# Decode attention over two caches: VectorE's work on the large cache as a hardware loop, each round's values loaded behind its own keys, strips summed in the loop

## The chip, the cores and the metric

The kernel runs on one core of a Trainium2 chip. The metric is the device time of one execution in microseconds (us). Between chips the kernel before moved from 1348.2 to 1349.3 us, so every experiment was timed beside runs of the kernel before on the same chip. All runs quoted are "fast", none of them over 1.5% above the fastest of its kernel.

Ratios are the mean time of one kernel's fast runs over that of the kernel before in the same rounds, so they are not quite the ratio of the medians that are quoted.

## The reference

Two independent attention blocks for a single query token, results concatenated. Block A ("the large cache") has 32 heads with 32 768 keys each; block B ("the small cache") has 32 query heads on 8 cache heads and looks at the last 4096 keys only.

```python
q = (x @ wq) per head                    # x: 1 x 512
scores = einsum("bhqd,bhkd->bhqk", q, k) * 128 ** -0.5
p = softmax(scores)
o = einsum("bhqk,bhkd->bhqd", p, v)
out = o.reshape(1, 1, 4096) @ wo         # A: 32 heads x 32768 keys; B: last 4096 keys, 8 cache heads
```

Every cache byte is used once: 2 x 268 MB for A, 2 x 8 MB for B, and four weight matrices of 4 MB, together 570 MB.

## The kernel before

In this kernel PE does the matrix products (19316 in the profiled run, its weight loads counted apart), VectorE and ScalarE the work on vectors (1664 and 169 instructions), GpSimd only some setting up (14), SyncE issues all loads but the two of x (1 KB each), and PSUM is the memory in which PE's results are placed.

The large cache is worked off in 32 rounds (16 pairs of heads, two halves of the keys each). One round needs two 4 MB loads of keys and two of values. There are two key buffers and two value buffers (slots), and all these loads are issued in order by SyncE. A round does this: PE transposes the keys in batches of eight 128x128 blocks, VectorE copies each batch out of PSUM, PE forms the scores; at the end of the round VectorE finds the maximum (a chain of about a dozen small operations), ScalarE takes the exponential, PE transposes the probabilities, ScalarE copies them, PE multiplies by the values, and VectorE adds the result to the running output, which lies in four strips of 32 partitions that have to be summed in the end.

In the kernel before this is software-pipelined: the value products of round i-1 run inside round i, so values are loaded one round behind their keys. PE's program is a hardware loop; VectorE's is straight code. The output weights are loaded last.

```python
WO_CUTS = {"A": (0, 16, 28, 32), "B": (0, 32)}        # pieces in which output weights are loaded
...
for i, (name, g, r) in enumerate(rounds):             # 32 rounds of the large cache
    self.loop = i if i >= 1 else None                 # a loop on PE only
    prev = [rounds[i - 1] + (u,) for u in range(2)]   # (i = 0: the small cache's two)
    for u in range(2):
        self.load_kv("k", name, g, r, u)              # keys of this round
        self.load_kv("v", *prev[u])                   # values of the round before
        hooks = {1: lambda: self.emit_PT(0)} if u == 0 else {}
        self.emit_unit(name, g, r, u, hooks)          # transposes, copies, scores
        self.emit_PV(*prev[u], pt=...)                # value products of the round before
    self.emit_round_end(name, g, r)                   # maximum, exponential
...
for u in range(2):
    self.load_kv("v", name, g, r, u)                  # values of the last round
for n in ("B", "A"):
    for part in range(len(self.WO_CUTS[n]) - 1):
        self.load_wo(n, part)
```

Of the kernel before, what the change touches and what calls it, by code (L numbers as in the profile page):

```python
# [9 lines left out]
DH = 128  # L10
# [26 lines left out]
class Op:  # L37
# [4 lines left out]



    __slots__ = ("eng", "fn", "deps", "take", "give", "loop", "signal", "count")

    def __init__(self, eng, fn, deps, take, give, loop):
        self.eng = eng
        self.fn = fn
        self.deps = [d for d in deps if d is not None]  # L50
        self.take = take
        self.give = give
        self.loop = loop
        self.signal = False
        self.count = None


class _Kernel:

    def __init__(self, nc, a, b, out):  # L60
# [30 lines left out]
        self.loop = None  # L91
# [3 lines left out]
    def op(self, eng, fn, *deps, take=(), give=None):  # L95
        o = Op(eng, fn, deps, list(take), give, self.loop if eng == "pe" else None)
        self.prog[eng].append(o)
        return o

    def build(self):  # L100
        nc = self.nc
        with nc.Block() as block:
            self.alloc()
            self.plan()
            for e in self.engines:
                for o in self.prog[e]:
                    for d in o.deps:
                        if isinstance(d, Op):
                            assert d.give is None
                            d.signal = True  # L110
            its = {}
            for o in self.prog["pe"]:
                if o.loop is not None:
                    assert not o.deps
                    its.setdefault(o.loop, []).append(o)
            for same in zip(*its.values(), strict=True):
                s = any(o.signal for o in same)
                for o in same:
                    o.signal = s
            for e in self.engines:  # L120
                n = 0
                for o in self.prog[e]:
                    if o.signal:
                        n += 1
                    o.count = n
            first = min(its) if its else None

            def emit_one(e, o, seen):
                need = {}
                for d in o.deps:  # L130
                    sem, val = (self.esem[d.eng], d.count) if isinstance(d, Op) else d
                    key = sem.name
                    if val > seen.get(key, 0) and val > need.get(key, (None, 0))[1]:
                        need[key] = (sem, val)
                for key, (sem, val) in need.items():
                    e.wait_ge(sem, val)
                    seen[key] = val
                for sem, n in o.take:
                    e.sem_inc(sem, -n)._wait_ge(sem, n)  # L139
                inst = o.fn(e)  # L140
                if o.give is not None:
                    inst.then_inc(o.give, 1)
                elif o.signal:
                    inst.then_inc(self.esem[o.eng], 1)

            def emit(eng_name):
                def body(e):
                    seen = {}
                    ops = self.prog[eng_name]
                    k = 0  # L150
                    while k < len(ops):
                        if ops[k].loop is None:
                            emit_one(e, ops[k], seen)
                            k += 1
                            continue
                        with e.Fori(0, len(its)):
                            for o in its[first]:
                                emit_one(e, o, seen)
                        k += sum(len(v) for v in its.values())
                return body  # L160

            block.gpsimd(emit("pool"))
            block.vector(emit("dve"))
            block.scalar(emit("act"))
            block.sync(emit("sp"))
            block.tensor(emit("pe"))

    def alloc(self):
# [6 lines left out]
        self.ptsb = [sb(f"ptsb{i}", [128, 512], BF16) for i in range(2)]  # L175
# [8 lines left out]
        for name, d in self.X.items():  # L184
# [3 lines left out]
                oc=sb(f"oc_{name}", [128, d["NG"], DH + 1], F32),  # L188
# [17 lines left out]
        self.qw = sb("qw", [128, 2, 64], BF16)  # L206
        ps = nc.alloc_psum_tensor
# [3 lines left out]
        self.ACC = [ps(f"psACC{i}", [128, 512], F32) for i in range(2)]  # L211
        s = nc.alloc_semaphore
        self.esem = {e: s(f"sem_{e}") for e in self.engines}
# [5 lines left out]
        self.t_copy = s("t_copy")  # L219
        self.t_exp = s("t_exp")  # L220
        self.t_q = s("t_q")
        self.t_pt = s("t_pt")
        self.t_acc = [s(f"t_acc{i}") for i in range(2)]
# [6 lines left out]
    def load_kv(self, which, name, g, r, u):  # L230
        d = self.X[name]
        slot = u if name == "A" else g
        buf, sem, free = ((self.kbuf, self.ksem, self.kfree) if which == "k" else (self.vbuf, self.vsem, self.vfree))
        h0 = g * d["kvg"] + u * d["kvu"]
        base = d["key0"] + d["blk"] * r
        src = d[which][0, h0:h0 + d["kvu"], base:base + d["blk"], :]
        src = src.rearrange("s (p j) d -> p s (j d)", p=128)
        dst = buf[slot][:, :].rearrange("p (s x) -> p s x", s=d["kvu"])
        self.load(dst, src, sem[slot], free[slot])

    def load_wq(self, name):
        slot = {"B": 0, "A": 1}[name]
        self.load(self.vbuf[slot][:, :], self.X[name]["wq"].rearrange("(p t) c -> p (t c)", t=4), self.vsem[slot],
                  self.vfree[slot])

    WO_CUTS = {"A": (0, 16, 28, 32), "B": (0, 32)}
    WO_SLOT = {"B": 0, "A": 1}

    def load_wo(self, name, part):
# [4 lines left out]
                  self.kfree[slot])  # L254
# [3 lines left out]
    def plan(self):  # L258
        self.kfree, self.vfree = [None, None], [None, None]
        self.nbatch = 0  # L260
        self.pending = []
        self.alphas = []
        self.fresh = True
# [8 lines left out]
        self.emit_unit("B", 0, 0, 0, {})  # L272
        self.emit_round_end("B", 0, 0)
        self.emit_unit("B", 1, 0, 0, {1: lambda: self.emit_PT(1)})
        self.emit_round_end("B", 1, 0)
        self.emit_qproj("A")
        self.emit_qcopy(0)

        rounds = [("A", i // a["R"], i % a["R"]) for i in range(self.NIT)]
        for i, (name, g, r) in enumerate(rounds):  # L280
            self.loop = i if i >= 1 else None
            if i == 0:
                prev = [("B", 0, 0, 0), ("B", 1, 0, 0)]
            else:
                prev = [rounds[i - 1] + (u,) for u in range(2)]
            for u in range(2):
                self.load_kv("k", name, g, r, u)
                self.load_kv("v", *prev[u])
                hooks = {1: lambda: self.emit_PT(0)} if u == 0 else {}
                self.emit_unit(name, g, r, u, hooks)  # L290
                self.emit_PV(*prev[u], pt=1 if i == 0 and u == 0 else 0)
            self.emit_round_end(name, g, r)
            if i + 1 < self.NIT:
                self.emit_qcopy(i + 1)
        self.loop = None
        name, g, r = rounds[-1]
        for u in range(2):
            self.load_kv("v", name, g, r, u)
# [3 lines left out]
        self.emit_PT(0)  # L302
        for n in ("B", "A"):
            self.emit_gather(n, 0, self.X[n]["NG"] - (n == "A"))
        self.emit_spread("B")
        for u in range(2):
            self.emit_PV(name, g, r, u, pt=0, final=True)
        self.emit_gather("A", a["NG"] - 1, a["NG"])
# [6 lines left out]
    def constants(self):  # L315
# [10 lines left out]
        for n in ("B", "A"):  # L326
            pool(lambda g, n=n: g.memset(c[n]["hsel"][:, :], 0.0))
            self.k_pool = pool(lambda g, n=n: g.memset(c[n]["b"][:, :], 0.0))
        dve = lambda fn, *deps, **k: self.op("dve", fn, *deps, **k)
        for i in range(2):  # L330
            dve(lambda v, i=i: v.memset(self.ACC[i][:, :], 0.0), give=self.t_acc[i])
# [18 lines left out]
    def emit_qproj(self, name):  # L350
        t = self.c[name]
        slot = {"B": 0, "A": 1}[name]
        ps, wq = self.ACC[slot], self.vbuf[slot]
# [8 lines left out]
        o = self.op("pe", mm, (self.xsem[name], 16), take=[(self.vsem[slot], 16), (self.t_acc[slot], 1)])  # L362
        self.vfree[slot] = o
        if name == "B":
            self.qready = self.op("dve", lambda v: v.tensor_copy(
                self.qz[:, 32:].rearrange("p (k w) -> p k w", w=32)[:, 0:8, 0:4],
                ps[:, 0:NQH].rearrange("p (k a) -> p k a", a=4)), o, self.k_pool)
        else:
            self.qready = self.op("dve", lambda v: v.tensor_copy(self.qa[:, :], ps[:, 0:NQH]), o)
        self.op("dve", lambda v: v.memset(self.m4[0:1, 0:1], 0.0), give=self.t_acc[slot])  # L370

    def emit_qcopy(self, i):
        g = i // self.X["A"]["R"]
# [230 lines left out]
```

## Time and profile before

Median 1348.19 us (1347.91 to 1348.41, three runs).

The kernel reads at 428 to 435 GB/s from the third slice to the 38th. At 432 GB/s, 570.4 MB take 1,320 us of the span of 1347.5 us.

The stage table of the end (columns: stretch, its length, busy us and instructions of PE, PE's weight loads, VectorE, ScalarE, GpSimd, then granted PE clock, DMA share, GB/s):

```profile
...
50.00:65.00 15.00, 7.35 (x166) 6.71 (x167) 5.46 (x19) 1.17 (x4) 0.00 (x0) 0.64 1.00 417
...
1295.00:1306.00 11.00, 8.41 (x238) 6.52 (x235) 9.47 (x24) 0.00 (x0) 0.00 (x0) 1.00 0.34 122
...
1333.00:1338.00 5.00, 5.00 (x22) 1.90 (x21) 0.00 (x0) 0.00 (x0) 0.00 (x0) 0.89 0.30 124
...
```

There is a hole (a stretch in which the mean DMA rate falls) between 1295 and 1306 us: 122 instead of 432 GB/s, which is 7.9 us of DMA time. It is there because SyncE's queue stands still at the last value load, whose buffer comes free only when the value product that starts at 1301.02 us is done, at 1303.0; the output weights, issued at 1303.39, stand behind it:

```profile
...
1301.02 1.96 PE L499 MATMUL psACC<-vbuf,ptsb 128*2 128x128 bf16 x128
...
1303.39 0.43 SPq L228 DMA_DIRECT2D kbuf<-in_B_wo_dram  x1
...
```

The timeline of one round (start, duration, engine, line, operation, tiles, count, and in brackets the idle time before it and what ended it):

```profile
...
623.34 3.57 PE L401 MATMUL psT<-ident,kbuf 128*128 128x128 bf16 x32 [7.37 <-PEq L139]
...
662.21 1.01 PE L401 MATMUL psT<-ident,kbuf 128*128 128x128 bf16 x8 [5.86 <-PEq L139]
```

The first transposes of two successive rounds' second halves are 38.87 us apart, which is four loads of 4.19 MB at 432 GB/s. Before each, PE stood idle (7.37 and 5.86 us; the sequencer, PEq, waited at the semaphore of the keys): the round waits for keys, and the kernel is bound by DMA. The end of the timeline:

```profile
...
1328.36 0.09 PEld L569 LDWEIGHTS psS<-kbuf,oz_B 128*1 128x1 bf16 x2 [2.73 <-DMA kbuf<-in_B_wo_dram]
...
1338.09 7.07 PE L569 MATMUL psPT<-kbuf,oz_A 128*1 128x512 bf16 x32
...
1345.20 0.68 DVE L573 CAST out_sb<-psPT 1x512 bf16<-1x512 f32 x1 [6.23 <-PE psPT L569]
```

The output projection of B starts when its 4 MB of weights have landed (1328.36), and that of A ends at 1345.2.

### The profile page before, as it was taken

The page shows a single profiled execution, that of the slowest core. Times are in us where ns is not written, and L with a number is a line of the kernel's source. Part 1 is how long each engine was busy: PE and PEld are TensorE (multiplying, and loading weights), DVE is VectorE, ACT ScalarE, POOL GpSimd, SP SyncE. Part 2 cuts the span into 40 slices and gives each one's busy share as a digit, 9 for nine tenths or more (in the row PEclk, how much of TensorE's full clock was granted, in tenths as well). Part 3 has the DMA queues.
Part 4 walks back from the last instruction along what each step waited for, and adds up shares of the span by engine and source line. Part 5 has one row for each costly group of instructions (what it writes and reads, how often), then busy time and mean ns, then how long its engine had stood idle before and what let it go on. Part 6 is the DMA issues. An engine that isn't in the chain of part 4 may idle for free. (4 is left out here: it accounts for less than half of the span.)

```text
span 1347.5 us, 42022 instructions
## 1 busy us (share of the span) xinstructions
PE 929.0 (69%) x19316; PEld 770.9 (57%) x19316; DVE 803.5 (60%) x1664; ACT 57.6 (4%) x169; POOL 2.0 (0%) x14
## 2 busy tenths in 40 slices
PE   3677766676577667667766775776677667667776
PEld 3556655565456556555655655565565556556553
DVE  3665755676565567556655765665675566557650
ACT  0000000000000000000000000000000000000000
POOL 0000000000000000000000000000000000000000
PEclk9888978888887888788878888877887888788778
DMA  9999999999999999999999999999999999999985
GB/s 400 422 429 428 431 433 429 433 432 432 429 433 432 433 430 430 434 432 430 432 432 431 431 433 432 431 430 433 432 433 428 434 432 430 430 435 431 431 337 254
DMA packets 21730, 570.81 MB, mean 424 GB/s; under 512 B 2498, under 2 KB 2500, under 8 KB 2628
## 3 DMA queue, kind: packets, MB, share of 16 engines
q1 hardware_dynamic: 21412, 570.44, 98.6%
q8 instruction: 15, 0.25, 0.1%
q14 instruction: 15, 0.12, 0.0%
q10 hardware_dynamic: 288, 0.00, 0.0%
HBM read 570.43 MB, written 0.00 MB: 423 GB/s over the span
## 5 line engine op out<-in xcount | busy, mean ns | idle before, releaser
L407 DVE COPY kt<-psT 128x1024 bf16<-128x1024 bf16 x1056 | 668.1, 685 | 385.6 <-PE psT L401 384.2
L401 PE MATMUL psT<-ident,kbuf 128*128 128x128 bf16 x8448 | 630.9, 245 | 370.3 <-PEq L139 366.0
L401 PEld LDWEIGHTS psT<-ident,kbuf 128*128 128x128 bf16 x8448 | 589.2, 112 | 469.3 <-issue 468.1
L431 PE MATMUL psS<-kt,qw 128*32 128x512 bf16 x2048 | 165.3, 401 | 0.0
L499 PE MATMUL psACC<-vbuf,ptsb 128*2 128x128 bf16 (+1 forms) x8256 | 132.1, 222 | 17.5 <-issue 14.9
L499 PEld LDWEIGHTS psACC<-vbuf,ptsb 128*2 128x2 bf16 (+1 forms) x8256 | 122.3, 85 | 35.6 <-issue 20.4
L466 ACT ACTIVATE psb<-psS,nb_A 128x512 bf16<-128x512 f32 x32 | 22.0, 688 | 971.6 <-DVE nb_A L464 971.6
L528 DVE SCALAR_TENSOR_TENSOR oc_A<-psACC,hot_A,oc_A 128x128 f32<-128x128 f32 x48 | 16.9, 351 | 62.9 <-PE psACC L499 62.9
L431 PEld LDWEIGHTS psS<-kt,qw 128*32 128x32 bf16 x2048 | 33.0, 96 | 25.4 <-issue 4.3
L482 ACT ACTIVATE ptsb<-psPT 128x512 bf16<-128x512 bf16 x34 | 20.3, 597 | 225.6 <-PE psPT L479 225.6
L451 DVE TENSOR_REDUCE tr_in<-psS 128x1 f32<-128x512 f32 x34 | 23.5, 691 | 4.5 <-PE psS L431 2.1
L453 DVE COPY m<-tr_a 1x16 f32<-1x16 f32 (+1 forms) x136 | 22.3, 164 | 2.6
L460 DVE COPY b_A<-mr_A 1x16 f32<-1x16 f32 x128 | 21.1, 165 | 2.4
L525 DVE TENSOR_SCALAR oc_A<-psACC,hot_A 128x128 f32<-128x128 f32 x16 | 5.6, 351 | 23.7 <-PE psACC L499 23.7
L479 PE MATMUL psPT<-ident,psb 128*128 128x128 bf16 x136 | 13.6, 224 | 4.3 <-PEq L139 4.3
L358 PE MATMUL psACC<-x_B,vbuf 128*128 128x1 bf16 x128 | 3.5, 165 | 13.6 <-PEq L139 13.6
L479 PEld LDWEIGHTS psPT<-ident,psb 128*128 128x128 bf16 x136 | 9.3, 100 | 4.7 <-issue 4.7
L569 PE MATMUL psS<-kbuf,oz_B 128*1 128x512 bf16 x32 | 9.9, 485 | 2.6 <-DMA kbuf<-in_B_wo_dram 2.6
L358 PEld LDWEIGHTS psACC<-x_B,vbuf 128*128 128x128 bf16 x128 | 3.5, 104 | 13.6 <-issue 13.6
L469 ACT ACTIVATE alpha_A<-cm_A,nb_A 128x1 f32<-128x1 f32 x32 | 9.0, 283 | 0.0
L569 PEld LDWEIGHTS psS<-kbuf,oz_B 128*1 128x1 bf16 x32 | 3.2, 102 | 8.9 <-issue 4.1
L573 DVE CAST out_sb<-psS 1x512 bf16<-1x512 f32 x1 | 0.7, 679 | 12.3 <-PE psS L569 12.3
(69 smaller groups left out, 104.6 us busy)
## 6 DMA issues: line engine op xcount, KB each, us to landing
kbuf<-in_A_k_cache_dram SPq DMA_DIRECT2D x64, 4096.0 KB, 27.9
vbuf<-in_A_v_cache_dram SPq DMA_DIRECT2D x64, 4096.0 KB, 35.3
kbuf<-in_B_k_cache_dram SPq DMA_DIRECT2D x2, 4096.0 KB, 27.7
vbuf<-in_B_v_cache_dram SPq DMA_DIRECT2D x2, 4096.0 KB, 25.5
vbuf<-in_B_wq_dram SPq DMA_DIRECT2D x1, 4096.0 KB, 12.5
vbuf<-in_A_wq_dram SPq DMA_DIRECT2D x1, 4096.0 KB, 41.7
kbuf<-in_B_wo_dram SPq DMA_DIRECT2D x1, 4096.0 KB, 24.9
kbuf<-in_A_wo_dram SPq DMA_DIRECT2D x1, 2048.0 KB, 29.3
```

The lines of the kernel that those rows point to most:

```text
L401: inst = e.transpose(T[:, 128 * k:128 * k + 128], src[:, DH * tile:DH * tile + DH], self.ident[:, :])
L407: self.op("dve", lambda v: v.tensor_copy(KT[:, :], T[:, :]), o, give=self.t_copy)
L431: inst = e.matmul(self.S[32 * c:32 * c + 32, :], lhsT=win, rhs=self.kt[(bb + c // 2) % NKT][:, 512 * (c % 2):512 * (c % 2) + 512], start=f ...
L451: o = dve(lambda v: v.reduce_max(tr["in"][:, 0:1], self.S[:, :], axis=AXX), sdone, self.k_pool)
L453: cps = [dve(lambda v, c=c: v.tensor_copy(m4[0:1, W * c:W * c + W], tr["a"][32 * c:32 * c + 1, 0:W]), o) for c in range(STRIPS)]
L460: x = dve(lambda v, c=c: v.tensor_copy(t["b"][32 * c:32 * c + 1, 0:W].rearrange("p (k h) -> p k h", k=KC), t["mr"][0:1, k, :].unsqueeze(1) ...
L466: self.op("act", lambda s: s.activation(out=self.psb[:, :], in_=self.S[:, :], func=ACTF.Exp, bias=t["nb"][:, k:k + 1], scale=self.SCALE, a ...
L479: inst = e.transpose(PT[:, 128 * jj:128 * jj + 128], self.psb[:, 128 * jj:128 * jj + 128], self.ident[:, :])
L482: self.op("act", lambda s: s.activation(out=pt[:, :], in_=PT[:, 0:512], func=ACTF.Copy), o, give=self.t_pt)
L499: inst = e.matmul(acc[32 * c:32 * c + HG, 0:w], lhsT=pt[:, col:col + HG], rhs=vv[:, :, 16 * kc + 4 * c + jj, :], start=(kc == 0 and jj == ...
L528: self.oop = dve(lambda v, src=src, hot=hot: v.scalar_tensor_tensor(out=oc, in0=src, scalar=hot, in1=oc, op0=ALU.mult, op1=ALU.add), pv, s ...
L569: inst = e.matmul(bank[0:1, 0:512], lhsT=t["oz"][:, a:a + 1], rhs=wo[:, 512 * a:512 * a + 512], start=(a == 0), stop=(a == 31), skip_group ...
```

## The change

Its intent: shorter programs. VectorE's work on the large cache becomes a hardware loop of 16 passes of two rounds (PE's loop has 32). To make all passes alike, the software pipeline is given up: a round loads its own values behind its own keys and multiplies by them at its end; the strips are summed ("gathered") on PE in every round, through a selection matrix (the window) that is zero except in the last round of a pair, so that every pass runs the same instructions and only a pair's finished output is added. One PSUM accumulator serves both halves instead of two. Each operation now sends its signal to one consumer only; if a second consumer needs it, a later operation of the same engine tells it. The output weights are cut finer.

```diff
-    WO_CUTS = {"A": (0, 16, 28, 32), "B": (0, 32)}
+    WO_CUTS = {"A": (0, 12, 22, 28, 32), "B": (0, 16, 32)}
...
-        self.emit_unit("B", 0, 0, 0, {})
-        self.emit_round_end("B", 0, 0)
-        self.emit_unit("B", 1, 0, 0, {1: lambda: self.emit_PT(1)})
-        self.emit_round_end("B", 1, 0)
-        self.emit_qproj("A")
...
+        for g in range(2):
+            self.emit_unit("B", g, 0, 0)
+            self.emit_round_end("B", g, 0)
+            if g == 0:
+                self.emit_qproj("A")
+            self.load_kv("v", "B", g, 0, 0)
+            self.emit_PV("B", g, 0, 0)
+            self.emit_gather("B", g, 0)
+        self.emit_spread("B")
+
+        for i in range(self.NIT):
+            g, r = divmod(i, a["R"])
+            self.loop = {"pe": i, "dve": g}
+            self.emit_qcopy(g)
             for u in range(2):
-                self.load_kv("k", name, g, r, u)
-                self.load_kv("v", *prev[u])
-                hooks = {1: lambda: self.emit_PT(0)} if u == 0 else {}
-                self.emit_unit(name, g, r, u, hooks)
-                self.emit_PV(*prev[u], pt=1 if i == 0 and u == 0 else 0)
-            self.emit_round_end(name, g, r)
...
+                self.load_kv("k", "A", g, r, u)
+                self.emit_unit("A", g, r, u)
+            self.emit_round_end("A", g, r)
+            for u in range(2):
+                self.load_kv("v", "A", g, r, u)
+                self.emit_PV("A", g, r, u)
+            self.emit_gather("A", g, r)
... (the emission of loops: waits relative to the pass, counters taken down at its end)
```

## The prediction

> **What bounds the kernel now.** The caches. The page counts 570.4 MB read from HBM, and the GB/s row holds 428 to 435 in every slice from the third to the 38th, with the DMA engines at 90% or more; at 432 GB/s that is 1,321 us of the 1,347.5 us span. The timeline shows a round of the large cache every 38.87 us (first transposes of two successive second units at 623.31 and 662.18), exactly four 4 MB loads. PE (69% busy) idles about 6 us per half round for keys. The rest of the span is: a start at 420 to 425 GB/s (about 5 us); a hole in the stage table between 1295 and 1306 us, worth about 7 us of DMA, because the last value load waits for the second value product of the round before (issued at 1303); and about 10 us after the last weights landed (1337.7), where the cold output projection still runs.
>
> **What the change does in steady state.** Bytes stay the same. A round becomes serial: its exponentials, transposed probabilities and value products no longer hide under the next round's transposes. Costed from the timeline: two units of transposes at the pace of the DVE copies, 12.2 + 9.8 us; last scores 0.8; maximum chain on DVE 3.3; exponential 0.9; transpose and copy of the probabilities 1.3; two value products 2.0 to 3.5 and 2.0, with a DVE hand-over of about 0.5 between (only one accumulator now); strip sum and gather about 1[...]. Sum 34.5 to 36.5 us, under DMA's 38.87: hidden. Value buffers must be free only some 48 us after the round's keys land, so the queue should not run dry.
>
> **Loops.** [...] Here PE stalled 3.6 and 4.3 us in the first pass of its loop body, and not in the second (135.94 us follows without a gap), so I expect cheap loop-backs.
>
> **Start.** The small cache's second value load waits for the gather after its first value product (one signal per PE operation, so the freed slot is told late), and the large cache's first keys queue behind it on the same issuing engine. WqA lands at 44 us, the first values at about 54, and the next load is issued at about 58 to 60: a new DMA hole of 6 to 8 us. Fetch stalls in the first loop pass may add about 2 us.
>
> **End.** The order keys, keys, values, values closes the 7 us hole: weights follow the values without a wait. The output projection is cut finer and follows the landing; I expect about 5 us from last landing to end, against 9.8.
>
> **Sum.** 1337.7 (last landing) - 7 + 7 + 2 + 5 + 0.7 (time over span) = about 1345 us, range 1338 to 1357. Faster by over 2% is nearly excluded by the DMA time (0.01); same 0.91; slower 0.08.
>
> **What would show it right or wrong.** GB/s still about 430 in the middle; round period 38.9 us, PE idle 2 to 4 us before a round's first transposes; a DMA hole near 53 to 60 us, none near 1295 to 1306; DVE busy about 800 us still; last landing to end about 5 us.
>
> **What would make it wrong.** If the serial chain exceeds 38.87 us (cold PE clock after each wait[...]), the bound moves from DMA to the chain and each extra microsecond per round costs 32 us: 1,375 us or more. If the hole at the start is smaller, or PE runs ahead, 1338 us.

The sum of the serial chain, 34.5 to 36.5 us, was made with one small term more than is printed, for the ends of the loops. What the prediction calls cold can be measured in the kernel before: B's output projection takes 9.89 us for 32 products, at a granted clock of 0.50 from 1328.36 to 1334.0 us, and A's 7.07 us for 32 at 1.00; the transposes at 623.34 us, after 7.37 us of idling, take 3.57 us for 32 at 0.50, those at 627.72 us 1.96 us at 1.00. What it calls fetch stalls are the stalls of 3.6 and 4.3 us: PE stands still from 111.9 to 115.5 us and from 128.3 to 132.6 us, and 16 KB fetches on q8 run from 113.0 to 114.1 and from 130.2 to 131.3 us. The 2 us for the changed kernel are the estimate, set below those two stalls.

## More of the kernel before

From the page of the profiled run: the span, the GB/s in 40 equal slices of it, and the queues with their packets, MB and share of the time of 16 DMA engines (q1 carries the loads; q8 and q14 carry instructions).

```profile
span 1347.5 us, 42022 instructions
...
GB/s 400 422 429 428 431 433 429 433 432 432 429 433 432 433 430 430 434 432 430 432 432 431 431 433 432 431 430 433 432 433 428 434 432 430 430 435 431 431 337 254
...
q1 hardware_dynamic: 21412, 570.44, 98.6%
q8 instruction: 15, 0.25, 0.1%
q14 instruction: 15, 0.12, 0.0%
...
```

Counted from the completion counts in the trace, the last weights land at 1338.1; the span ends 9.4 us later.

## The result, and the profile after

Median 1341.95 us (1341.74 to 1342.04, four runs) against 1348.3 us; ratio 0.9953, 95% interval 0.9936 to 0.9970. The measured time lies in the stated range. What the page of the changed kernel says:

```profile
span 1340.3 us, 41412 instructions
...
GB/s 397 303 437 428 433 428 434 431 432 432 427 436 428 434 432 428 435 429 434 429 432 433 430 434 429 433 432 429 435 429 432 433 429 433 431 432 430 431 434 353
...
q8 instruction: 10, 0.16, 0.1%
...
q14 instruction: 5, 0.04, 0.0%
...
```

The middle still runs at 427 to 437 GB/s. The second slice has fallen from 422 to 303 GB/s, the last two have risen from 337 and 254 to 434 and 353. Fetches on q14 fell from 15 to 5. The stage table:

```profile
...
50.00:65.00 15.00, 9.36 (x100) 6.32 (x100) 5.10 (x10) 0.00 (x0) 0.00 (x0) 0.57 0.42 164
...
1295.00:1306.00 11.00, 11.00 (x182) 8.36 (x180) 11.00 (x20) 0.00 (x0) 0.00 (x0) 1.00 1.00 429
...
1333.00:1338.00 5.00, 4.67 (x21) 1.59 (x20) 0.00 (x0) 0.00 (x0) 0.00 (x0) 1.00 0.43 174
...
```

The hole at 1295 us is gone and there is a new one between 50 and 65 us, 164 GB/s, which is 9.3 us of DMA time. Its cause can be read in the timeline of SyncE's issues and PE:

```profile
...
30.70 29.20 SPq L291 DMA_DIRECT2D vbuf<-in_B_v_cache_dram  x2
...
44.24 3.55 PE L422 MATMUL psACC<-x_A,vbuf 128*128 128x1 bf16 x128 [2.58 <-DMA vbuf<-in_A_wq_dram]
...
54.03 3.59 PE L553 MATMUL psACC<-vbuf,ptsb 128*16 128x512 bf16 x32 [6.23 <-DMA vbuf<-in_B_v_cache_dram]
...
59.23 0.74 PE L596 MATMUL psG<-oc_B,hsel_B 128*32 128x1 f32 x4 [1.61 <-DVE oc_B L582]
...
59.94 0.51 SPq L291 DMA_DIRECT2D kbuf<-in_A_k_cache_dram  x1
...
```

"30.70 29.20 SPq ... x2" is a merged line: the first value load of the small cache is issued at 30.7 us, the second at 59.5. In between SyncE waits, and the large cache's first keys stand behind it, though their buffer is free. The slot of the second value load was read last by A's query projection, done at 47.8 us; but that operation signals VectorE, and SyncE hears of it only from the first product of the gather (59.23). A round in the middle:

```profile
...
627.20 6.52 PE L463 MATMUL psT<-ident,kbuf 128*128 128x128 bf16 x64 [4.61 <-DMA kbuf<-in_A_k_cache_dram]
...
649.58 0.40 PE L486 MATMUL psS<-kt,qw 128*32 128x512 bf16 x4 [0.47 <-DVE kt L466]
653.98 0.61 PE L528 MATMUL psPT<-ident,psb 128*128 128x128 bf16 x4 [4.00 <-ACT psb L518]
655.28 3.58 PE L553 MATMUL psACC<-vbuf,ptsb 128*2 128x128 bf16 x128 [0.69 <-ACT ptsb L531]
659.32 2.43 PE L553 MATMUL psACC<-vbuf,ptsb 128*2 128x128 bf16 x128 [0.46 <-DVE oc_A L579]
662.38 0.44 PE L596 MATMUL psG<-oc_A,hw 128*32 128x1 f32 x4 [0.63 <-DVE oc_A L582]
666.05 1.12 PE L463 MATMUL psT<-ident,kbuf 128*128 128x128 bf16 x17 [3.23 <-DMA kbuf<-in_A_k_cache_dram]
```

From the first transposes (627.20) to the end of the gather (662.8) the serial chain takes 35.6 us; PE then waits 3.2 us for the next keys, and the period is 38.85 us as before. From the view of waits, over the whole run (engine, line, what it waited for: us in total, times, longest):

```profile
...
PE psT L463 <- DMA kbuf<-in_A_k_cache_dram: 126.1, 30, 5.2
...
```

That is 4.2 us of slack in each of the 30 waits. The end:

```profile
...
1323.00 7.37 PE L625 MATMUL psS<-kbuf,oz_B 128*1 128x512 bf16 x32
1330.45 2.75 PE L625 MATMUL psPT<-kbuf,oz_A 128*1 128x512 bf16 x12
1333.53 4.48 PE L625 MATMUL psPT<-kbuf,oz_A 128*1 128x512 bf16 x20 [0.34 <-DMA kbuf<-in_A_wo_dram]
```

B's projection starts at 1323.0, without waiting, and A's follows its pieces. The last weights land at 1336.6 (before: 1338.1), and the span ends 3.7 us later (before: 9.4).

So far the account looks like the prediction's. One number does not fit. A hole of 9.3 us opened and one of 7.9 us closed, so the last landing should have come about 1.4 us later; it came 1.5 us earlier. The DMA engines got 3 us from somewhere.

### The profile page after: what moved, and what is told of

Read it like the earlier page. It is cut to its first block, busy times and chain, and to the rows that moved or that the text cites. A ratio compares the mean times of both kernels' runs of the same rounds, so it can differ in the third digit from the quotient of the medians.

```text
span 1340.3 us, 41412 instructions
## 1 busy us (share of the span) xinstructions
PE 958.2 (71%) x19416; PEld 773.7 (58%) x19416; DVE 791.7 (59%) x1662; ACT 61.2 (5%) x201; POOL 2.0 (0%) x15
## 4 chain that ended last, share of the span: by engine, by line
DMA 64%; PE 26%; issue 0%; DVE 0%; SPq 0%
DMA kbuf<-in_A_k_cache_dram 62%; PE psT L463 22%; PE psS L486 4%; DMA kbuf<-in_A_wo_dram 2%; PE psPT L625 0%; DVE out_sb L629 0%; SPq L291 0%
## 5 line engine op out<-in xcount | busy, mean ns | idle before, releaser
L466 DVE COPY kt<-psT 128x1024 bf16<-128x1024 bf16 x1056 | 655.7, 684 | 211.1 <-PE psT L463 208.9
L463 PE MATMUL psT<-ident,kbuf 128*128 128x128 bf16 x8448 | 576.5, 234 | 135.7 <-DMA kbuf<-in_A_k_cache_dram 126.1
L463 PEld LDWEIGHTS psT<-ident,kbuf 128*128 128x128 bf16 x8448 | 537.1, 106 | 227.7 <-DMA kbuf<-in_A_k_cache_dram 134.0
L553 PE MATMUL psACC<-vbuf,ptsb 128*2 128x128 bf16 (+1 forms) x8256 | 190.5, 273 | 45.4 <-ACT ptsb L531 22.0
L553 PEld LDWEIGHTS psACC<-vbuf,ptsb 128*2 128x2 bf16 (+1 forms) x8256 | 170.5, 106 | 66.7 <-ACT ptsb L531 30.5
L486 PE MATMUL psS<-kt,qw 128*32 128x512 bf16 x2048 | 157.6, 385 | 15.2 <-DVE kt L466 15.2
L528 PE MATMUL psPT<-ident,psb 128*128 128x128 bf16 x136 | 20.7, 307 | 139.3 <-ACT psb L518 139.3
L528 PEld LDWEIGHTS psPT<-ident,psb 128*128 128x128 bf16 x136 | 11.7, 130 | 149.4 <-ACT psb L518 149.4
L596 PE MATMUL psG<-oc_A,hw 128*32 128x128 f32 (+1 forms) x128 | 14.1, 220 | 22.1 <-DVE oc_A L582 19.4
L596 PEld LDWEIGHTS psG<-oc_A,hw 128*32 128x32 f32 x128 | 6.5, 109 | 27.3 <-issue 27.3
L565 DVE TENSOR_SCALAR oc_A<-oc_A,alpha_A 128x129 f32<-128x129 f32 x16 | 4.6, 289 | 16.5 <-ACT alpha_A L521 16.5
```

The source lines that it names most:

```text
L463: inst = e.transpose(T[:, 128 * k:128 * k + 128], src[:, DH * tile:DH * tile + DH], self.ident[:, :])
L466: self.copies.append(self.op("dve", lambda v: v.tensor_copy(KT[:, :], T[:, :]), o, to="pe"))
L486: inst = e.matmul(self.S[32 * c:32 * c + 32, :], lhsT=win, rhs=self.kt[(bb + c // 2) % NKT][:, 512 * (c % 2):512 * (c % 2) + 512], start=f ...
L528: inst = e.transpose(PT[:, 128 * jj:128 * jj + 128], self.psb[:, 128 * jj:128 * jj + 128], self.ident[:, :])
L553: inst = e.matmul(acc[32 * c:32 * c + HG, 0:w], lhsT=pt[:, col:col + HG], rhs=vv[:, :, 16 * kc + 4 * c + jj, :], start=(kc == 0 and jj == ...
L596: self.gath = self.op("pe", lambda e, c=c, c2=c2: e.matmul(self.G[0:32, c0 + c:c0 + c2], lhsT=win, rhs=t["oc"][:, c:c2], start=False, stop ...
```

## The experiments

The first theory was the prediction's: the time is DMA time plus holes in it, plus what runs after the last landing. VectorE's loop as such is worth nothing, since rounds wait for DMA. Rival theories stand with each run below.

### 1. Does VectorE's loop matter? (changed kernel, VectorE straight)

```diff
-            self.loop = {"pe": i, "dve": g}
+            self.loop = {"pe": i}
```

> The changed kernel with the VectorE work as straight code again, PE still a loop. Theory (VectorE's loop saves and costs nothing, since the rounds are bound by DMA): 1342 us, within 1 us; instruction bytes on the instruction queues up by about 0.1 MB. Rival (the loop itself brought the gain, by taking instruction fetches off the DMA engines or by its branches): over 2 us away from 1342.

Measured: 1352.16 us (1352.03 to 1352.26), ratio 1.0023 (1.0006 to 1.0039), so 10.2 us more than the changed kernel and slower than the kernel before. The theory fell, except that the instruction bytes rose as expected. A line of the queues on its page, and then a stage table of its end:

```profile
...
q14 instruction: 16, 0.13, 0.0%
...
```

```profile
...
1334.00:1338.00 4.00, 4.00 (x22) 1.63 (x23) 0.19 (x1) 0.00 (x0) 0.00 (x0) 1.00 0.33 134
1338.00:1342.00 4.00, 4.00 (x20) 1.59 (x19) 0.68 (x1) 0.00 (x0) 0.00 (x0) 1.00 0.06 25
1342.00:1346.00 4.00, 4.00 (x20) 1.52 (x19) 0.00 (x0) 0.00 (x0) 0.00 (x0) 1.00 0.06 26
...
```

Eleven more fetches, 0.09 MB more; and at the end a DMA share of 0.06 for 8 us. The share is the mean over the 16 DMA engines, so one of them, busy alone, is 1/16 = 0.06. The last loads of the run are held up by a single DMA engine.

In the traces each load of caches and weights shows 16 completions, at different times, and the kernel waits for all 16 (`take=[(self.ksem[slot], 16)]`). So the last one counts: in the kernel before, the 15th completions of three loads of keys came at 619.07, 638.51 and 657.93 us, the 16th at 623.05, 642.49 and 661.92 us, and PE's transposes started at 623.34, 642.62 and 662.21 us. This gives a measure of the lag: how far the 15th and the 16th completion of a load fall behind its median one. Computed from the completion times in the traces, for the load nearest to each time:

```
load at about             100 us   400 us   700 us  1000 us  1250 us   last weights
before         16th        +0.5     +2.6     +5.6     +8.6    +11.5     +3.6 us
               15th        +0.4     +1.6     +1.6     +1.6     +1.6
after          16th        +1.6     +1.1     +1.2     +1.1     +1.0     +0.9
               15th        +1.5     +1.1     +1.2     +1.0     +1.0
VectorE        16th        +1.8     +2.0     +4.9     +7.9    +10.4    +10.3
straight       15th        +1.4     +0.9     +0.9     +0.9     +0.6
```

In the kernel before, one engine falls behind the other 15 all through the run, to 11.5 us, and every load, and so every round, waits for it. The GB/s row cannot show it, because the 15 others work on ahead, by the end more than a whole load further into the queue (11.5 us, where the median completions of successive loads are 9.7 us apart). In the changed kernel the lag stays at 1 us. With VectorE's code straight it is back: 9.4 us more lag at the end, for 11 more fetches.

The lag does not drift, it grows in steps, and the steps come with the fetches. In the kernel before, the fetch packets on q14 start at 328, 424, 525, 620, 721, 828, 932, 1025, 1128 and 1224 us. At each of these ten times the 16th completion falls 0.95 to 1.03 us further behind, from 1.62 us before the first to 11.46 us after the last; between them it does not move by more than 0.06 us, and the 15th stays at 1.6 us all along. With VectorE straight in the changed kernel, ten steps of 0.6 to 1.0 us do the same between 351 and 1242 us. So nearly all of the lag comes from single fetches, and since the 15th does not follow, they hit the same engine each time. The other five fetches on q14 in the kernel before (at 43, 141, 228, 330 and 736 us) do not add to it, nor do the five that the changed kernel has: the change took away just the ten that do.

And the hole at the end of the kernel before was not lost time for that engine. Its stage table, closer:

```profile
...
1297.00:1300.00 3.00, 3.00 (x54) 2.47 (x52) 3.00 (x6) 0.00 (x0) 0.00 (x0) 1.00 0.18 76
1300.00:1302.00 2.00, 2.00 (x92) 1.67 (x93) 1.82 (x4) 0.00 (x0) 0.00 (x0) 1.00 0.04 16
...
```

The share falls through 0.18 to 0.04. While the other engines stood still, the slow one worked off its lag: 11.5 us before the hole, 3.6 us after it, and 11.5 - 3.6 is the 7.9 us of the hole. It never ran dry: its part of the value load before landed at 1308.9 us, 5.9 us after SyncE had issued the last one.

The hole may itself come from the lag. The value product at 1301 that SyncE waits for needs values whose 16th completion came at 1299.2 us, the median one at 1287.7. No run took the lag away and left the rest of the kernel before as it was, so this is not shown.

### 2. Is it VectorE that slows, or the DMA engine? (changed kernel, idle ScalarE padded)

A rival to "fetches hold up a DMA engine" is that VectorE itself runs slower in straight code. So fetches were added on an engine that has nothing to do: 40 tiny ScalarE instructions per round, which touch no data of the kernel.

```diff
+            for _ in range(40):
+                self.pad = self.op("act", lambda s: s.activation(
+                    out=self.scratch[:, :], in_=self.ident[:, 0:1], func=ACTF.Copy), getattr(self, "pad", None))
... (and one line that allocates the scratch tile)
```

> The changed kernel, with 40 tiny ScalarE instructions added in straight code at the end of every round, where ScalarE idles for over 30 us. They touch no data of the kernel and lie on no chain. Theory (each fetch of 8 KB of instructions holds up one of the 16 DMA engines by about 1 us, and a load is done only when its slowest engine is): 10 to 20 more fetches on the instruction queue, the 16th completion of a load falls 10 us or more behind the median one by the end, and the time rises by 8 us or more, to 1350 us or more. Rival (in the straight VectorE code it was VectorE itself that got slower, not the DMA engine): 1342 us, spread of the completions still about 1 us.

Measured: 1348.31 us (1347.88 to 1348.41) against 1341.94 for the unchanged changed kernel on the same chip: 6.4 us more.

```profile
...
q14 instruction: 16, 0.12, 0.0%
...
```

Eleven more fetches; the 16th completion fell from 1.5 us behind the median at 400 us (the 15th: 1.1) to 7.2 us at the end (the 15th: 1.0), 6.3 us more than the 0.9 us of the changed kernel, which is the time that was lost. The direction of the expectation held, and the rival is out, since nothing on VectorE or PE was touched. The pages of the changed kernel and of experiment 1 say so too: VectorE's copies take 684 ns each in a loop and in straight code.

```profile
...
L466 DVE COPY kt<-psT 128x1024 bf16<-128x1024 bf16 x1056 | 655.7, 684 | 211.1 <-PE psT L463 208.9
...
```

```profile
...
L466 DVE COPY kt<-psT 128x1024 bf16<-128x1024 bf16 x1056 | 656.8, 684 | 226.4 <-PE psT L463 224.1
...
```

The size did not hold: at least 8 us was expected, from about 1 us for each fetch. Here most steps of the lag are 0.64 to 0.68 us, against about 0.98 us with VectorE's fetches. Both are more than the 0.31 to 0.33 us that an 8 KB fetch packet itself lasts in the traces of the kernel before and the changed one; why they cost more, and why one more than the other, stays open.

### 3. Closing the hole at the end alone (kernel before, B's weights ahead of the last value load)

```diff
-        for u in range(2):
-            self.load_kv("v", name, g, r, u)
-        for n in ("B", "A"):
-            for part in range(len(self.WO_CUTS[n]) - 1):
-                self.load_wo(n, part)
+        self.load_kv("v", name, g, r, 0)
+        self.load_wo("B", 0)
+        self.load_kv("v", name, g, r, 1)
+        for part in range(len(self.WO_CUTS["A"]) - 1):
+            self.load_wo("A", part)
```

> The kernel before with the small cache's output weights issued ahead of the last value load, which waits for its buffer until 1303 us. Theory (the hole of 7.9 us near 1295 to 1306 us is an issue-order wait, and it is one part of what the change gained): DMA stays near 430 GB/s there, last landing comes about 8 us earlier, and since the output projection still runs after it on PE for about 17 us, the time falls by 4 to 7 us, to 1341 to 1344 us. Rival (the end is set by PE's chain from the last keys): no change, 1348 us.

Measured: 1353.25 us (1352.09 to 1354.33), ratio 1.0034 (1.0017 to 1.0051): slower, against both what the theory and what its rival said. The hole did close (431 to 439 GB/s from 1295 to 1306 us). But:

```profile
...
1326.00:1330.00 4.00, 1.65 (x64) 1.68 (x68) 0.00 (x0) 0.00 (x0) 0.00 (x0) 0.50 0.22 90
1330.00:1334.00 4.00, 2.92 (x84) 2.11 (x73) 0.99 (x4) 0.00 (x0) 0.00 (x0) 0.66 0.09 33
1334.00:1338.00 4.00, 4.00 (x20) 1.56 (x19) 0.05 (x1) 0.00 (x0) 0.00 (x0) 1.00 0.05 20
...
```

```profile
...
1328.35 3.58 PE L499 MATMUL psACC<-vbuf,ptsb 128*2 128x128 bf16 x128 [11.96 <-PEq L139]
...
```

The tail of one engine working alone is back at the end (DMA shares of 0.09 and 0.05), and the last landing is at 1337.8 us against 1338.1 in the kernel before: filling the hole brought nothing, which fits an engine that had never paused in it. Its lag on the last weights is 11.2 us instead of 3.6. And the last values, now behind 4 MB more, landed at 1328.1 instead of 1318.6 us, so that PE's last products began at 1328.35 instead of 1318.87 and both projections ran later. So the hole of 7.9 us was worth about nothing while the lag was there.

### 4. What the finer weight cuts bring (changed kernel, the old cuts)

```diff
-    WO_CUTS = {"A": (0, 12, 22, 28, 32), "B": (0, 16, 32)}
+    WO_CUTS = {"A": (0, 16, 28, 32), "B": (0, 32)}
```

> The changed kernel with the cuts of the output weights of the kernel before (one piece for the small cache, 16, 12 and 4 columns for the large one). Theory (the finer cuts are worth part of the 5 us between last landing and end): PE waits about 4 us more for the first piece, and the end comes 3 to 5 us later, 1345 to 1347 us. Rival (the cuts bring nothing, only the closed hole does): 1342 us.

Measured: 1346.84 us (1346.17 to 1347.45), ratio 0.9984 (0.9968 to 1.0001): 4.9 us more than the changed kernel by the medians, 4.2 us by the ratios. Here the theory held. In the timeline PE waits 2.1 us for the whole of B's weights, begins B's projection at 1326.6 instead of 1323.0 us, and then runs both projections without a break, until 1342 us:

```profile
...
1326.62 8.75 PE L625 MATMUL psS<-kbuf,oz_B 128*1 128x512 bf16 x32 [2.09 <-DMA kbuf<-in_B_wo_dram]
1335.21 7.07 PE L625 MATMUL psPT<-kbuf,oz_A 128*1 128x512 bf16 x32
```

### 5. How much slack has the serial round? (both kernels, a longer chain)

The first step of the maximum chain, 0.69 us on VectorE, is repeated n more times in every round of the large cache.

```diff
         o = dve(lambda v: v.reduce_max(tr["in"][:, 0:1], self.S[:, :], axis=AXX), self.sdone, self.k_pool)
+        for _ in range(n if name == "A" else 0):
+            o = dve(lambda v: v.reduce_max(tr["in"][:, 0:1], self.S[:, :], axis=AXX), o)
```

n = 3 in the changed kernel:

> The changed kernel with the first step of the maximum chain of the large cache (0.69 us on VectorE) done three more times in every round, so that the serial chain is about 2.2 us longer. Theory (PE waits 4.2 us per round for keys, so the chain has that much slack): the time stays at 1342 us, within 1.5 us, and PE's wait for keys falls to about 2 us per round. Rival (the serial chain already sets the pace): 2.2 x 32, about 70 us more.

Measured: 1343.1 us, ratio 0.9955 (0.9938 to 0.9971), where the changed kernel had 0.9953: no cost. PE's wait for keys fell from 126.1 us in total to 80.5, which is 2.9 us for each wait, where about 2 had been expected:

```profile
...
PE psT L463 <- DMA kbuf<-in_A_k_cache_dram: 80.5, 28, 3.6
...
```

n = 10 in the changed kernel:

> The same with ten more, about 7.2 us longer. Theory (slack of about 4 us per round): the bound moves from DMA to the chain, the rest of about 3 us per round shows, 60 to 100 us more, so 1400 to 1440 us, and the DMA rate falls to about 400 GB/s. Rival (the slack is larger, because the queue of loads absorbs it): under 20 us more.

Measured: 1422.62 us (1420.7 to 1422.98), ratio 1.0546. That is 81 us more than the changed kernel, 2.5 us per round, out of 7.2 added: the slack is about 4.7 us per round, close to the 4.2 us of the waits. As expected, the bound has moved, and the DMA rate fell in nearly every slice:

```profile
...
GB/s 398 314 435 409 385 429 412 401 411 402 406 406 413 430 399 410 403 410 403 408 434 399 413 400 413 400 412 413 419 411 400 412 400 413 400 437 406 406 403 211
...
```

n = 10 in the kernel before:

> The kernel before with the same ten more steps per round (7.2 us). Theory (there the chain lies under the next round's transposes, and PE and VectorE idle about 12 us per round waiting for keys): 1348 us, within 4 us. Rival (the kernel before had no more slack than the changed one): 60 to 100 us more, as in the changed kernel.

Measured: 1354.96 us (1354.46 to 1358.24), ratio 1.0050 (1.0033 to 1.0067): 5.7 us more, a little outside the 4 us expected, but far from 60. In the two profiled runs (spans of 1353.5 and 1347.5 us) 2.5 us of it is a later last landing, 1340.6 against 1338.1, and 3.5 us comes after it, 12.9 against 9.4. One chain at the end of the run hides under nothing, and the longer code also costs three more fetches on q14 (18 against 15), with a lag of up to 12.2 us; which of them makes which part was not tested. So the change gave up most of the slack of a round. On this DMA-bound case that cost nothing, but it is the price of the simpler loop.

### 6. The hole at the start

Two different edits that should close it: issue the large cache's first keys ahead of the small cache's second values,

```diff
             self.load_kv("v", "B", g, 0, 0)
+            if g == 0:
+                self.load_kv("k", "A", 0, 0, 0)
... (and this load is left out of the first round)
```

> The changed kernel, with one load moved: the large cache's first keys are issued before the small cache's second values, which in the changed kernel they stand behind. Theory (the time is DMA time plus holes; the new hole at 52 to 61 us, 9.3 us of DMA by the stage table, is an issue-order wait): the hole goes, the profile shows about 430 GB/s through 50 to 65 us, last landing about 1327, time about 1333 us against 1342. Rival (the start is held by the late round 0, so the hole only moves to the first round of the large cache): about 1342 us, with a hole between 60 and 130 us.

or leave the order and tell SyncE early, by a tiny product on PE right after A's query projection:

```diff
         self.free["v"][slot] = o
+        if name == "A":
+            self.op("pe", lambda e: e.matmul(self.G[0:32, 500:501], lhsT=self.ident[:, 0:32],
+                    rhs=self.ident[:, 0:1], start=False, stop=True, skip_group_check=True), to="sp")
```

> The changed kernel, order of loads unchanged, but one tiny matrix product after the large cache's query projection tells the issuing engine at once that the slot is free, instead of the gather 12 us later. Theory (the hole is the late signal): the second small value load is issued at about 48 us instead of 60, the hole goes, time about 1333 to 1334 us, the same as with the moved load. Rival (the hole comes from something else, such as the first pass of the code): no change, 1342 us.

Measured: 1337.62 us (ratio 0.9917) and 1339.29 us (ratio 0.9924). Both close the hole at 50 to 65 us (428 and 435 GB/s there), so its cause is as stated, the late signal and the order of issue. But both bring half of what was expected. The stage table of the moved load shows why:

```profile
...
50.00:65.00 15.00, 9.16 (x124) 5.75 (x125) 5.91 (x12) 0.00 (x0) 0.00 (x0) 0.72 1.01 428
...
100.00:135.00 35.00, 24.83 (x495) 20.67 (x488) 17.94 (x40) 1.77 (x6) 0.00 (x0) 0.76 0.90 380
...
```

Between 100 and 135 us a second hole opened, 380 GB/s or 4.2 us of DMA time here, and 362 GB/s or 5.7 us with the early signal. Here both theory and rival were half right. The rounds of the large cache start when PE is done with the small cache, at 84 us, some 20 us after their first keys have landed (the moved load); SyncE hears only at 123 us that the first value buffer is free, later than the DMA queue runs empty. In the moved load's run the last 3.2 us before that are a stall of PE ahead of its first gather (119.99 to 123.15 us) that ended with no wait in the profile, so part of this hole may be the stall in the first loop pass that the prediction spoke of; it was not separated.

So the start was reordered as a whole: the early signal, the keys issued early, and the small cache's second key unit transposed before its first value products instead of after them.

```diff
+        self.emit_unit("B", 0, 0, 0)
+        self.emit_round_end("B", 0, 0)
+        self.emit_qproj("A")                    # with the early signal
+        for g in range(2):
+            self.load_kv("v", "B", g, 0, 0)
+        self.load_kv("k", "A", 0, 0, 0)
+        self.emit_unit("B", 1, 0, 0)
         for g in range(2):
-            self.emit_unit("B", g, 0, 0)
-            self.emit_round_end("B", g, 0)
-            if g == 0:
-                self.emit_qproj("A")
-            self.load_kv("v", "B", g, 0, 0)
+            if g == 1:
+                self.emit_round_end("B", 1, 0)
             self.emit_PV("B", g, 0, 0)
             self.emit_gather("B", g, 0)
... (and this load is left out of the first round)
```

> The changed kernel with the start reordered: early signal for the freed slot, large cache's first keys issued before the rounds start, and the small cache's second key unit transposed before the first value products rather than after them. Theory (moving the load alone left a second hole of 4 us of DMA between 100 and 135 us, because the rounds start 20 us after their first keys have landed): both holes go, about 430 GB/s from 5 us on, time 1332 to 1334 us. Rival (the second hole has another cause): 1337 us, as with the load moved alone.

Measured: 1334.42 us (1333.96 to 1334.54), ratio 0.9889 (0.9872 to 0.9905); the changed kernel beside it 1341.94 us. The stage table:

```profile
...
50.00:65.00 15.00, 11.50 (x181) 8.41 (x179) 12.37 (x27) 0.00 (x0) 0.00 (x0) 0.95 1.03 430
...
100.00:135.00 35.00, 25.49 (x506) 21.28 (x507) 17.61 (x39) 1.77 (x6) 0.00 (x0) 0.76 1.01 432
...
```

Both holes are gone, and the time is just above the 1332 to 1334 us expected. The start hole of the changed kernel is thus worth 7.5 us of time.

The unaltered changed kernel was run once more on that chip, for comparison:

> The changed kernel, unaltered, on the chip of the runs below. About 1342 us, 0.995 of the kernel before.

Measured: 1341.94 us (1341.82 to 1342.2), ratio 0.9945 (0.9929 to 0.9962).

Last, the same reordered start with the large cache's weights in seven pieces, `"A": (0, 10, 18, 24, 28, 30, 32)`:

> The same with the large cache's output weights in seven pieces instead of four, the last ones smaller. Theory (about ten products are left when the last weights land): up to 1 us less, 1331 to 1333 us. Rival (more loads cost as much as they bring): the same or slower.

Measured: 1333.61 us (1333.54 to 1334.99), ratio 0.9887 (0.9870 to 0.9903). Against 0.9889 this is no clear difference, so neither the up to 1 us expected nor its rival is shown. It and the reordered start are the best versions found: faster than both kernels, and 1.1% faster than the one before.

## Why the prediction was right, and where it was not

The time was within the range (1345 predicted, 1341.95 measured), and the change was under 2%, as forecast. The picture of the middle held, and that was insight. That the sum came out was luck: it has two large terms wrong, which nearly cancel. It took 7 us off the last landing for a hole that gave nothing back, and nothing for the lag, which gave back 10.6 us.

- **Bound by DMA; the longer serial chain is hidden: right.** The period stayed at 38.85 us. The chain was put at 34.5 to 36.5 us and measured 35.6. Part of it is PE at a lower clock: the granted clock is 0.50 from 653.98 to 658.9 us, after a wait of 4.0 us, and the first value product (655.28) takes 3.58 us, against 1.96 us at a clock of 1.00 for the same 128 products in the kernel before (634.93). Experiment 5 shows the slack from both sides.
- **"A new DMA hole of 6 to 8 us" at the start: right in cause, a little small.** It is 9.3 us of DMA, worth 7.5 us of time (experiment 6).
- **"Fetch stalls in the first loop pass may add about 2 us": not seen as time.** PE stalled once, 2.7 us, before the large cache's first gather (a 16 KB fetch on q8 ran from 120.9 to 121.9 us in that time), and no DMA hole followed in the changed kernel (432 GB/s from 100 to 135 us). Nor did the loops fetch in every pass: PE's 32 and VectorE's 16 passes stand beside 10 fetches on q8 in the whole run, the last at 277 us, and 5 on q14.
- **"Closes the 7 us hole", counted as -7: this step failed.** The hole was read off the table as lost DMA time. For 15 of 16 DMA engines it was; for the slowest it was the time in which it caught up. Experiment 3 closed it alone and moved the last landing by 0.3 us.
- **VectorE's loop, counted as 0: this step failed too.** The prediction asked only whether the loops would stall an engine. It did not ask which loads the fetches hold up. Taking ten of them away (15 to 5 on the page) kept one DMA engine from falling 11.5 us behind; undoing the loop alone costs 10.2 us by the medians, 9.4 by the ratios (experiment 1).
- **Finer weight cuts, about -5 after the last landing: right.** 9.4 us became 3.7; experiment 4 gives 4 to 5 us for the cuts.

The sum in the measured terms: loop about -10, cuts -4 to -5, start hole +7.5, which makes about -7, against -6.4 measured; the closed hole at the end is not needed in it. In landings: the lag that the kernel before still had to pay (7.9 us worked off in the hole and 3.6 at the end, 11.5) became 0.9, the hole at the start added 9.3, so the last landing should move by 9.3 - 10.6 = -1.3 us; it moved by -1.5. These terms were measured one at a time, each against the changed kernel, and need not add exactly.

What stays open: why a fetch holds an engine up longer (0.6 to 1.0 us) than its packet lasts (0.3 us), why ScalarE's fetches cost less than VectorE's, whether the hole at the end came from the lag, and what makes the 5.7 us of the longer chain in the kernel before.

## What to carry to other kernels

In a kernel bound by DMA like this one, look at the slowest DMA engine, not at the mean: PE started here only after the 16th completion of a load, up to 11.5 us behind the median one, ten instruction fetches had held up one engine by about 0.98 us each, and 0.1 MB of straight code cost 10 us in 1340, which neither the GB/s row nor the share of the instruction queues (0.0%) showed. Here a DMA share near 1/16 at the end of a run (0.06 for 8 us in experiment 1), and a 16th completion that drifted away from the 15th (11.5 us behind the median against 1.6), gave it away. Before counting a hole in the mean DMA rate as a gain, ask whether the slowest engine idled in it: in the hole of 7.9 us here it did not. And ask when a slot's reader tells its loader: here it told it 11.7 us after it was done (59.5 against 47.8 us), and the large cache's first keys, behind it in the issue queue, waited as well.
